# Top-32 attention and a cosine-gated feed-forward layer on one core: feed-forward blocks of 128 tokens, shared PSUM banks, mask and Exp first in ScalarE's slot

## The chip, the cores and the metric

The kernel runs on one NeuronCore of a Trainium2 chip. The core has five engines that run side by side, each through its own instructions in order: TensorE (PE: matmuls; its weight loads are listed as PEld), VectorE (DVE), ScalarE (ACT), GpSimd (POOL) and SyncE (SP, which here issues DMAs). They wait for each other through semaphores. The metric is the device time of one execution in microseconds, the median of several runs.

## What is computed

Eight batches of eight heads, 576 queries and keys of 64 dimensions. Of each row of scores the 32 largest go through a softmax, the others count as zero. The output of all heads, as 4608 tokens of 512 features, goes through a layer of 2048 hidden units that are gated by their own cosine. All data are float32.

```python
def _attn_ref(q, k, v):                      # (8, 8, 576, 64)
    scores = scale * np.matmul(q, k.transpose(0, 1, 3, 2))
    kth = np.partition(scores, -top_k, axis=-1)[..., -top_k:-top_k + 1]
    scores = np.where(scores >= kth, scores, -1000000000.0)
    scores = scores - np.max(scores, axis=-1, keepdims=True)
    attn = np.exp(scores)
    attn = attn / (np.sum(attn, axis=-1, keepdims=True) + 1e-09)
    return np.matmul(attn, v).astype(np.float32)

def _moe_ref(x, w_in, w_out):                # (4608, 512), (512, 2048), (2048, 512)
    h = x @ w_in
    g = h * np.cos(h)
    return (g @ w_out).astype(np.float32)
```

## The kernel before

**Units and slots.** The tokens of all batches stand in a row and are cut into 36 tiles of 128. A unit is one such tile for one pair of heads, so there are 4 x 36 = 144 units, four to a tile (`units`). A tile that crosses from one batch to the next has two `parts`. The main loop runs slot by slot: slot i does the top-k of unit i on VectorE, and other steps for its neighbours. Slots 0 to 8 are written in `early_slot`, the others in `slot`. The kernel is scheduled by hand: each engine runs its instructions in the order in which the code issues them.

**A unit's way.** `scores` (L206) makes 2 x 128 x 576 scores on TensorE in four PSUM banks (`sc`), one slot ahead; `take_scores` (L216) copies them to `s` on ScalarE. `topk_round` (L230, L233) finds eight maxima at a time on VectorE, four rounds for each head. One slot later `bounds`, `mask` and `exponentials` (L241, L244, L253, L261, L266) run on ScalarE: everything below the 32nd value is pushed far down, Exp is taken and its sum goes to `den`. In the slot after that `reciprocal` (L270) stands first on VectorE, and GpSimd normalises (L275) and splits the words into halves (L287), which SP writes to DRAM (L292). One slot later SP issues a DMA that reads them back transposed into `pT` (L298), and one slot later still `values` (L333) multiplies by V on TensorE into the bank `o`, and `take_values` (L340) copies the result to `xT` on ScalarE. The first eight units are transposed on TensorE instead (`transposes_now`, L310, with copies L314 and L317).

**Feed-forward.** `widths` cuts the tokens into blocks: four of 128, fifteen of 256, two of 128. When all units of a block are through, its products may start. A call of `ff1` (L381) makes 256 columns of the first product in a bank `mm`: for a block of 256 one group of hidden units, for one of 128 two groups. Each matmul of the program is two instructions in the trace. When a bank is full, `take_first` (L393) copies it to `g` on ScalarE. The cosine is taken as a sine: GpSimd reduces the argument (L419 to L428), ScalarE takes the sine (L438, with a table load when Exp was last), and GpSimd multiplies (`gate`, L445). A call of `ff2` (L457) adds two groups of hidden units to a bank `o` of its own (`o2`), which `take_second` (L466) copies to `ob` for the output's DMA. Which calls stand in a slot is decided when the program is built, by `feed`: four credits a slot, alternating between the two products, if their inputs were issued early enough.

**PSUM.** Eight banks: four for `sc`, two that take turns for `mm`, one for `o` and one for `o2`.

**Weights.** They come as chunks of 64-bit words that are decoded on ScalarE (L126 to L128), VectorE (L137, L138) and GpSimd (L147, L148) in the first slots.

**The end.** After the last unit four more slots let it pass through, and a last loop feeds what is left of the products; there VectorE takes over the reduction and the gate.

Of the kernel before, what the change touches and what calls it, by code (L numbers as in the profile page):

```python
# [17 lines left out]
P = 128  # L18
# [13 lines left out]
def kernel(  # L32
# [58 lines left out]
    for f in range(NF):  # L91
        w = consts.tile([P, DM], F32, tag=f"w_out{f}", name=f"w_out{f}")
        w_out.append(w)
        chunks.append((moe_w_out[f * P : (f + 1) * P, :], w))
    CHUNKS, XB = 8, 4
    ff = {"live": 0, "tick": 0, "now": 0, "credit": 0.0, "end": False, "kind": 0}
# [205 lines left out]
    def transposes_now(u):  # L302

        s = u.pop("s").rearrange("p j k -> p (j k)")
        tp = ps.tile([P, 2, 2, 512], F32, tag="sc", name="tp", bufs=1)
        tt = ps.tile([P, 512], F32, tag="ot", name="tt", bufs=1)
        for c in range(2 * NT + 1):
# [11 lines left out]
    def values(u):  # L319

        pT = u.pop("pT")
        o = u["o"] = ps.tile([P, 512], F32, tag="ot", name="o", bufs=1)
        for b, _, rows, r0 in u["parts"]:
            st = pairs[b, u["hp"]]
            r = slice(r0, r0 + rows)
            for c in range(NT + 1):
                for j in range(2):
                    d = slice(j * D, (j + 1) * D)
                    if c < NT:
                        lhsT, rhs = st["v"][:, c, d], pT[:, j * (NT + 1) + c, r]  # L330
                    else:
                        lhsT, rhs = st["v_tail"][:, d], pT[:, NT, r]
                    nc.tensor.matmul(o[d, r], lhsT, rhs, start=c == 0, stop=c == NT)  # L333

    def take_values(u):
        blk = block_of[u["tok"]]
        if "xT" not in blk:
            blk["xT"] = work.tile([P, NP, blk["w"]], F32, tag="xT", name="xT", bufs=4)
        at = u["tok"] - blk["t0"]
# [3 lines left out]

    widths = [P] * 4 + [2 * P] * (B * S // (2 * P) - 3) + [P] * 2
    assert sum(widths) == B * S
    blocks, block_of = [], {}
# [20 lines left out]
    def ff1(blk, i):  # L367
# [6 lines left out]
        if part % 2 == 0:  # L374
            blk["mm"] = ps.tile([P, 512], F32, tag="mm", name="mm")
        g, mm = blk["g"][-1], blk["mm"]
# [71 lines left out]
    def ff2(blk, i, f0):  # L448
        w = blk["w"]
        if f0 == 0:  # L450
            blk["o"] = ps.tile([P, 512], F32, tag="o2", name="o2", bufs=1)
        o = blk["o"]
# [71 lines left out]

    EARLY = 2 * NP

    def early_slot(i, u, w):
        n = 3 if i < 6 else 2
        decode_second()
        topk_round(u, 0)  # L530
# [9 lines left out]
        topk_round(u, 1)  # L540
        topk_round(u, 2)
        topk_round(u, 3)
        decode_third(1)
# [9 lines left out]
        if i != NP:  # L553
            decode_first(n - 1)
        feed(2)
        if w:
            transposes_now(w)
        decode_first(n - len(wq["second"]))
        if w:
            values(w)  # L560
            take_values(w)
        sines(2)

    def slot(i, u, w, x, y, z):
        decode_second()
        if x:
            reciprocal(x)
        if u:
            for rnd in range(TOPK // 8):
                topk_round(u, rnd)  # L570
        take_banks()
# [14 lines left out]
        if x:  # L586
            normalise(x)
            split(x)
            write_halves(x)
        if w:  # L590
            bounds(w)
            mask(w)
            exponentials(w)
        feed(2)
        take_banks()
        decode_third(2)
        decode_first(2)
        reduce_first()
        reduce_second()
        feed(4)  # L600
        sines(2)

    tt = ps.tile([P, 512], F32, tag="ot", name="warm", bufs=1)
    for _ in range(8):
# [7 lines left out]
    decode_first(3)  # L612
    for i in range(NU + 4):
        ff["end"] = i >= NU
        ff["credit"] = min(ff["credit"] + 4.0, 5.0)
        ff["now"] += 1
        wq["ready"] = wq["done"]
        u, w = (units[i - n] if 0 <= i - n < NU else None for n in range(2))
        x, y, z = (units[i - n] if EARLY <= i - n < NU else None for n in range(2, 5))
        if i <= EARLY:  # L620
# [50 lines left out]
```

## Time and profile before

| | us |
|---|---|
| runs before (3) | median 1688.67, 1683.35 to 1691.39 |
| the profiled execution | 1690.27 |
| its span, first to last instruction | 1688.4 |
| TensorE busy | 1483.0 (88%) |
| VectorE busy | 1457.4 (86%) |
| ScalarE busy | 1110.4 (66%) |
| GpSimd busy | 1100.0 (65%) |
| mean granted TensorE clock | 0.935 of 2.4 GHz |

The profile lists each instruction with its start and length, and for an idle stretch of an engine the instruction elsewhere that ended it. Two engines are busy for most of the span, so a share of busy time alone doesn't tell which of them sets the pace: that is read from who waits for whom in the stretch where the kernel spends most of its time. Matmuls are pipelined, and a busy TensorE is therefore not one at its peak; what a group of matmuls costs is read from the start of the group to the start of the next. TensorE's clock has two levels, 1.2 and 2.4 GHz, and the granted clock of a stretch is given as a share of the higher one.

### The profile page before, as it was taken

To read this page: it belongs to the slowest core of one execution; us is meant where nothing else is said; L and a number is where in the kernel's file an instruction comes from. 1 tells how busy PE (TensorE), PEld (TensorE's weight loads), DVE (VectorE), ACT (ScalarE), POOL (GpSimd) and SP (SyncE) were. 2 spreads that over 40 slices of the span, in tenths; PEclk is the share of its full clock that TensorE was granted. 3 is DMA by queue.
4 is the path that set the end of the run, shared out by engine and by line. 5 is a ranking of instruction groups with operands and counts; after the bars stand their busy time and mean duration, and the time that the engine had idled before them with its cause. 6 is when DMAs were issued, how large, how long until landed. Compare 5 with 4: busy or idle time off the path is not lost.

```text
span 1688.4 us, 24574 instructions
## 1 busy us (share of the span) xinstructions
PE 1483.0 (88%) x8400; PEld 967.1 (57%) x8400; DVE 1457.4 (86%) x3107; ACT 1110.4 (66%) x2200; POOL 1100.0 (65%) x835
## 2 busy tenths in 40 slices
PE   4658679797989999999999989999999999999998
PEld 2546356373646565656565646565656565656674
DVE  6999998899899898989898988989898989898620
ACT  7878657566667676767676766666676767676520
POOL 5787666476486767676767676767676767676600
PEclk9689789797999999999999999999999999999999
DMA  8422464435544465546454355544553454443500
GB/s 258 134 76 80 119 161 132 129 114 165 140 132 121 105 175 140 140 105 175 136 144 118 106 145 150 146 119 133 147 147 107 129 149 133 120 127 111 134 13 19
DMA packets 381502, 216.57 MB, mean 128 GB/s; under 512 B 330688, under 2 KB 347073, under 8 KB 381377
## 3 DMA queue, kind: packets, MB, share of 16 engines
q1 hardware_dynamic: 381216, 214.84, 46.3%
q8 instruction: 66, 1.08, 0.3%
q14 instruction: 60, 0.48, 0.1%
q10 hardware_dynamic: 160, 0.16, 0.0%
HBM read 45.09 MB, written 89.65 MB: 80 GB/s over the span
## 4 chain that ended last, share of the span: by engine, by line
PE 67%; ACT 14%; DVE 6%; DMA 4%; POOL 4%; issue 3%; SPq 2%; ACTq 0%; POOLq 0%; DVEq 0%
PE o L457 26%; PE mm L381 23%; PE o L333 10%; PE sc L206 8%; DMA pT<-rows 4%; ACT s L261 3%; ACT s L253 3%; DVE m L230 3%; ACT s L216 2%; DVE rest L233 2%; ACT ob L466 1%; ACT nd L244 1%; POOL g L445 1%; POOL halves L287 1%; POOL x L428 1%
## 5 line engine op out<-in xcount | busy, mean ns | idle before, releaser
L457 PE MATMUL o<-w_out,g 128*128 128x512 f32 x1152 | 592.3, 652 | 110.7 <-ACT ob L466 81.9
L230 DVE MAX8 m<-rest 128x8 f32<-128x576 f32 x864 | 609.4, 747 | 0.0
L381 PE MATMUL mm<-xT,w_in 128*128 128x256 f32 (+1 forms) x2688 | 544.7, 355 | 9.0 <-ACT xT L340 4.6
L381 PEld LDWEIGHTS mm<-xT,w_in 128*128 128x128 f32 x2688 | 458.8, 194 | 143.5 <-issue 86.8
L457 PEld LDWEIGHTS o<-w_out,g 128*128 128x128 f32 x1152 | 224.8, 206 | 374.1 <-issue 250.7
L233 DVE MATCH_REPLACE8 rest<-m,rest 128x576 f32<-128x576 f32 x576 | 423.4, 743 | 0.0
L275 POOL TENSOR_SCALAR s<-s,rden 128x576 f32<-128x576 f32 x288 | 212.1, 749 | 166.4 <-DVE rden L270 164.5
L287 POOL COPY halves<-s 128x2304 uint16<-128x2304 uint16 x136 | 285.9, 2102 | 30.9 <-DMA rows<-halves 23.6
L445 POOL TENSOR_TENSOR g<-g,x 128x1024 f32<-128x1024 f32 x65 | 153.7, 2365 | 219.3 <-ACT x L438 219.2
L216 ACT COPY s<-sc 128x1152 f32<-128x1152 f32 x144 | 161.1, 1119 | 125.5 <-PE sc L206 117.1
L261 ACT ACTIVATE s<-s,nd 128x576 f32<-128x576 f32 x288 | 219.3, 762 | 0.6
L233 DVE MATCH_REPLACE8 rest<-m,s 128x576 f32<-128x576 f32 x288 | 211.6, 743 | 0.0
L333 PE MATMUL o<-pT,v 128*64 128x128 f32 (+1 forms) x2560 | 170.0, 278 | 40.6 <-DMA pT<-rows 26.2
L253 ACT ACTIVATE s<-s,nb 128x576 f32<-128x576 f32 x288 | 205.3, 760 | 0.0
L230 DVE MAX8 m<-s 128x8 f32<-128x576 f32 x288 | 201.7, 742 | 0.0
L206 PE MATMUL sc<-k,q 64*128 64x288 f32 (+1 forms) x1280 | 192.1, 447 | 7.7 <-DMA k<-in_k_dram 7.6
L333 PEld LDWEIGHTS o<-pT,v 128*64 128x64 f32 x2560 | 135.3, 143 | 108.2 <-issue 64.2
L340 ACT COPY xT<-o 128x128 f32<-128x128 f32 x144 | 37.9, 263 | 240.6 <-PE o L333 240.6
L393 ACT ACTIVATE g<-mm 128x512 f32<-128x512 f32 x144 | 84.1, 586 | 128.9 <-PE mm L381 128.9
L428 POOL TENSOR_TENSOR x<-g,x 128x1024 f32<-128x1024 f32 x67 | 158.3, 2363 | 5.6
L270 DVE RECIPROCAL rden<-den 128x2 f32<-128x2 f32 x144 | 22.3, 155 | 131.8 <-ACT den L266 131.8
L206 PEld LDWEIGHTS sc<-k,q 64*128 64x128 f32 (+1 forms) x1280 | 104.3, 185 | 53.1 <-issue 18.6
(48 smaller groups left out, 1059.7 us busy)
## 6 DMA issues: line engine op xcount, KB each, us to landing
rows<-halves SPq DMA_DIRECT2D x136, 576.0 KB, 3.1
q<-in_q_dram SPq DMA_DIRECT2D x32, 288.0 KB, 3.1
out_dram<-ob SPq DMA_DIRECT2D x36, 256.0 KB, 2.7
st<-in_moe_w_in_dram SPq DMA_DIRECT2D x16, 512.0 KB, 6.2
v<-in_v_dram SPq DMA_DIRECT2D x32, 256.0 KB, 3.0
st<-in_moe_w_out_dram SPq DMA_DIRECT2D x16, 512.0 KB, 3.3
k<-in_k_dram SPq DMA_DIRECT2D x31, 144.0 KB, 3.3
k<-in_k_dram SPq DMA_DIRECT2D x32, 128.0 KB, 3.7
```

Of the source, the lines that this page charges most:

```text
L206: nc.tensor.matmul(sc[r0 : r0 + rows, j, h, 0:HS], st["q"][d, q0 : q0 + rows], st["k"][d, h * HS : (h + 1) * HS], start=True, stop=True,)
L216: nc.scalar.copy(out=s.rearrange("p j (h w) -> p (j h) w", h=2), in_=u.pop("sc").rearrange("p j h w -> p (j h) w")[:, :, 0:HS],)
L230: nc.vector.max(m8[:, j, at], src[:, j])
L233: nc.vector.match_replace(rest[:, j], m8[:, j, at], src[:, j], NEG)
L253: nc.scalar.activation(out=s[:, j], in_=s[:, j], func=AF.Prelu, bias=nb[:, j, 1:2], scale=SCALE, alpha=FAR)
L261: nc.scalar.activation(out=s[:, j], in_=s[:, j], func=AF.Exp, bias=nd[:, j : j + 1], scale=1.0, accum_out=den[:, j : j + 1],)
L275: nc.gpsimd.tensor_scalar(out=s[:, j], in0=s[:, j], scalar1=rden[:, j : j + 1], scalar2=1.0, op0=ALU.mult, op1=ALU.mult,)
L287: nc.gpsimd.tensor_copy(out=halves, in_=s.rearrange("p (k h) -> p h k", h=2))
L333: nc.tensor.matmul(o[d, r], lhsT, rhs, start=c == 0, stop=c == NT)
L381: nc.tensor.matmul(mm[:, at : at + w], w_in[f // FC][:, c, (f % FC) * P : (f % FC + 1) * P], blk["xT"][:, c], start=c == 0, stop=c == NC - 1,)
L428: nc.gpsimd.tensor_tensor(out=x, in0=g, in1=x, op=ALU.subtract)
L457: nc.tensor.matmul(o, g[:, at : at + P], w_out[f], start=f == 0, stop=f == NF - 1)
```

## The change

All feed-forward blocks are 128 tokens wide. The PSUM banks of `mm`, `o`, `o2` and of the ninth transpose (`tt`) come from one group of four. In `slot`, mask and Exp of the last unit stand after the first round of the top-k, so first on ScalarE. The last four units (from `LAST`) are masked, normalised, transposed on TensorE and multiplied with V in one slot, and the main loop ends three slots earlier. A slot's credits are 4.1, and its last call of `feed` is for one call. There are nine buffers for `g` and staged weights, and five for `xT`. In `early_slot` the decoding on VectorE in slot 0 comes after the third round, and `feed` stands after the transposes.

```diff
@@ -92,7 +92,7 @@
         w = consts.tile([P, DM], F32, tag=f"w_out{f}", name=f"w_out{f}")
         w_out.append(w)
         chunks.append((moe_w_out[f * P : (f + 1) * P, :], w))
-    CHUNKS, XB = 8, 4
+    CHUNKS, XB = 9, 4
     ff = {"live": 0, "tick": 0, "now": 0, "credit": 0.0, "end": False, "kind": 0}
 
     wq = {"next": 0, "loaded": deque(), "second": deque(), "third": deque(), "done": 0, "ready": 0}
@@ -303,7 +303,7 @@
 
         s = u.pop("s").rearrange("p j k -> p (j k)")
         tp = ps.tile([P, 2, 2, 512], F32, tag="sc", name="tp", bufs=1)
-        tt = ps.tile([P, 512], F32, tag="ot", name="tt", bufs=1)
+        tt = ps.tile([P, 512], F32, tag="mm", name="tt", bufs=4)
         for c in range(2 * NT + 1):
             j, k = divmod(c, NT + 1)
             to = tt[:, 0:P] if c == NT else tp[:, 0, j, k * P : (k + 1) * P]
@@ -319,7 +319,7 @@
     def values(u):
 
         pT = u.pop("pT")
-        o = u["o"] = ps.tile([P, 512], F32, tag="ot", name="o", bufs=1)
+        o = u["o"] = ps.tile([P, 512], F32, tag="mm", name="o", bufs=4)
         for b, _, rows, r0 in u["parts"]:
             st = pairs[b, u["hp"]]
             r = slice(r0, r0 + rows)
@@ -335,14 +335,13 @@
     def take_values(u):
         blk = block_of[u["tok"]]
         if "xT" not in blk:
-            blk["xT"] = work.tile([P, NP, blk["w"]], F32, tag="xT", name="xT", bufs=4)
+            blk["xT"] = work.tile([P, NP, blk["w"]], F32, tag="xT", name="xT", bufs=5)
         at = u["tok"] - blk["t0"]
         nc.scalar.copy(out=blk["xT"][:, u["hp"], at : at + P], in_=u.pop("o")[:, 0:P])
         blk["left"] -= 1
 
 
-    widths = [P] * 4 + [2 * P] * (B * S // (2 * P) - 3) + [P] * 2
-    assert sum(widths) == B * S
+    widths = [P] * (B * S // P)
     blocks, block_of = [], {}
     t0 = 0
     for w in widths:
@@ -372,7 +371,7 @@
             blk["g"].append(ffw.tile([P, 1024], F32, tag="g", name="g", bufs=CHUNKS))
             ff["live"] += 1
         if part % 2 == 0:
-            blk["mm"] = ps.tile([P, 512], F32, tag="mm", name="mm")
+            blk["mm"] = ps.tile([P, 512], F32, tag="mm", name="mm", bufs=4)
         g, mm = blk["g"][-1], blk["mm"]
         for a in range(nf):
             f = i * nf + a
@@ -448,7 +447,7 @@
     def ff2(blk, i, f0):
         w = blk["w"]
         if f0 == 0:
-            blk["o"] = ps.tile([P, 512], F32, tag="o2", name="o2", bufs=1)
+            blk["o"] = ps.tile([P, 512], F32, tag="mm", name="o2", bufs=4)
         o = blk["o"]
         per = 1024 // w
         for f in range(f0, f0 + 2):
@@ -522,11 +521,12 @@
 
 
 
-    EARLY = 2 * NP
+    EARLY, LAST = 2 * NP, NU - NP
 
     def early_slot(i, u, w):
         n = 3 if i < 6 else 2
-        decode_second()
+        if i > 0:
+            decode_second()
         topk_round(u, 0)
         scores(units[i + 1])
         for load, b, hp in at_slot.get(i, []):
@@ -539,6 +539,8 @@
             reciprocal(w)
         topk_round(u, 1)
         topk_round(u, 2)
+        if i == 0:
+            decode_second()
         topk_round(u, 3)
         decode_third(1)
         if w:
@@ -552,22 +554,34 @@
         reduce_second()
         if i != NP:
             decode_first(n - 1)
-        feed(2)
         if w:
             transposes_now(w)
+        feed(1)
         decode_first(n - len(wq["second"]))
         if w:
             values(w)
             take_values(w)
+        feed(2)
         sines(2)
 
     def slot(i, u, w, x, y, z):
+        now = w and i - 1 >= LAST
         decode_second()
         if x:
             reciprocal(x)
         if u:
-            for rnd in range(TOPK // 8):
-                topk_round(u, rnd)
+            topk_round(u, 0)
+        if w:
+            bounds(w)
+            mask(w)
+            exponentials(w)
+        if u:
+            topk_round(u, 1)
+            topk_round(u, 2)
+        if now:
+            reciprocal(w)
+        if u:
+            topk_round(u, 3)
         take_banks()
         if z:
             values(z)
@@ -587,20 +601,23 @@
             normalise(x)
             split(x)
             write_halves(x)
-        if w:
-            bounds(w)
-            mask(w)
-            exponentials(w)
         feed(2)
         take_banks()
         decode_third(2)
         decode_first(2)
+        if now:
+            normalise(w)
         reduce_first()
         reduce_second()
-        feed(4)
+        feed(2)
+        if now:
+            transposes_now(w)
+            values(w)
+            take_values(w)
+        feed(1)
         sines(2)
 
-    tt = ps.tile([P, 512], F32, tag="ot", name="warm", bufs=1)
+    tt = ps.tile([P, 512], F32, tag="mm", name="warm", bufs=4)
     for _ in range(8):
         nc.tensor.transpose(tt[:, 0:P], ident, ident)
     load_qk(0, 0)
@@ -610,13 +627,13 @@
     scores(units[0])
     take_scores(units[0])
     decode_first(3)
-    for i in range(NU + 4):
+    for i in range(NU + 1):
         ff["end"] = i >= NU
-        ff["credit"] = min(ff["credit"] + 4.0, 5.0)
+        ff["credit"] = min(ff["credit"] + 4.1, 5.0)
         ff["now"] += 1
         wq["ready"] = wq["done"]
         u, w = (units[i - n] if 0 <= i - n < NU else None for n in range(2))
-        x, y, z = (units[i - n] if EARLY <= i - n < NU else None for n in range(2, 5))
+        x, y, z = (units[i - n] if EARLY <= i - n < LAST else None for n in range(2, 5))
         if i <= EARLY:
             early_slot(i, u, w)
         else:
```

On TensorE in the steady part, the slot in which a second product ends or starts. `sc` are the scores, `mm` the first product, `o_8085<-w_out` a second product (`o` with a number), `o<-pT,v` P@V. Before:

```order
L333 MATMUL o<-pT,v 64x128 x8
L333 MATMUL o<-pT,v_tail_116 64x128 x2
L206 MATMUL sc<-k,q 128x288 x4
L457 MATMUL o_7771<-w_out_104,g 128x512
L457 MATMUL o_7771<-w_out_105,g 128x512
L457 MATMUL o_8085<-w_out_90,g 128x512
L457 MATMUL o_8085<-w_out_91,g 128x512
L457 MATMUL o_8085<-w_out_92,g 128x512
L457 MATMUL o_8085<-w_out_93,g 128x512
```

After the change:

```order
L333 MATMUL o<-pT,v 64x128 x8
L333 MATMUL o<-pT,v_tail_112 64x128 x2
L206 MATMUL sc<-k,q 128x288 x4
L380 MATMUL mm<-xT,w_in_86 128x128 x16
L456 MATMUL o_8218<-w_out_90,g 128x512
L456 MATMUL o_8218<-w_out_91,g 128x512
L380 MATMUL mm<-xT,w_in_87 128x128 x8
L456 MATMUL o_8218<-w_out_92,g 128x512
L456 MATMUL o_8218<-w_out_93,g 128x512
```

Where one second product followed directly on another, two calls of the first product of a new block now stand between the scores and the start of the next second product.

On ScalarE in the steady part, around the copy of a finished second product to `ob`. Before:

```order
L340 COPY xT<-o 128x128
L216 COPY s<-sc 128x1152
L241 ACTIVATE nb<-m_5715 128x4
L244 ACTIVATE nd<-m_5715,nb 128x1 x2
L253 ACTIVATE s<-s,nb 128x576 x2
L261 ACTIVATE s,den<-s,nd 128x576 x2
L266 ACTIVATE den<-den,eps 128x2
L466 ACTIVATE ob<-o_5545 128x512
L393 ACTIVATE g<-mm 128x512
```

After the change:

```order
L216 COPY s<-sc 128x1152
L437 ACT_TABLE_LOAD
L437 ACTIVATE x<-x,halfpi 128x1024
L241 ACTIVATE nb<-m_6345 128x4
L244 ACTIVATE nd<-m_6345,nb 128x1 x2
L253 ACTIVATE s<-s,nb 128x576 x2
L261 ACT_TABLE_LOAD
L261 ACTIVATE s,den<-s,nd 128x576 x2
L266 ACTIVATE den<-den,eps 128x2
L465 ACTIVATE ob<-o_6146 128x512
L340 COPY xT<-o 128x128
L216 COPY s<-sc 128x1152
```

The group from `nb` to `den` stood behind `xT` and `s` of its slot and now stands ahead of them; `ob` and `xT` follow on it.

On VectorE, the start of the program. Before:

```order
L69 MEMSET eps 128x1
L137 TENSOR_SCALAR w_in_86<-w_in_86 128x512
L138 TENSOR_SCALAR w_in_86<-w_in_86 128x512
...
L230 MAX m_171<-s 128x8 x2
L233 MATCH_REPLACE rest<-m_171,s 128x576 x2
```

After the change:

```order
L69 MEMSET eps 128x1
L230 MAX m_165<-s 128x8 x2
L233 MATCH_REPLACE rest<-m_165,s 128x576 x2
L230 MAX m_165<-rest 128x8 x2
L233 MATCH_REPLACE rest<-m_165,rest 128x576 x2
...
L137 TENSOR_SCALAR w_in_86<-w_in_86 128x512
```

The decoding of the first weights (three pairs of L137 and L138) moved behind the third round of unit 0.

## Rows read from the trace of the kernel before

**Rows 1.** Stretch, length, busy PE PEld DVE ACT POOL, granted clock, DMA share, GB/s.

```profile
236.00:1583.00 1347.00, 1226.36 (x6922) 790.50 (x6923) 1226.83 (x2645) 913.61 (x1817) 925.67 (x685) 0.95 0.49 134
```

**Rows 2.** Timeline of VectorE: start, duration, instruction, [idle before <-what ended it].

```profile
760.03 0.17 DVE L270 RECIPROCAL rden<-den 128x2 f32<-128x2 f32 x1 [6.04 <-ACT den L266]
...
1554.08 1.40 DVE L230 MAX8 m<-s 128x8 f32<-128x576 f32 x2
...
1563.78 1.40 DVE L230 MAX8 m<-s 128x8 f32<-128x576 f32 x2
```

**Rows 3.** Waits, 236 to 1583 us: total, times, longest; VectorE's, then TensorE's.

```profile
DVE rden L270 <- ACT den L266: 120.1, 49, 6.9
...
PE o L457 <- ACT ob L466: 71.7, 26, 3.8
PE o L333 <- DMA pT<-rows: 26.0, 14, 7.2
```

**Rows 4.** Timeline around 750 us, ScalarE's rows and then TensorE's.

```profile
742.16 0.58 ACT L466 ACTIVATE ob<-o 128x512 f32<-128x512 f32 x1
742.76 1.28 ACT L438 ACT_TABLE_LOAD   x1
744.05 1.15 ACT L438 ACTIVATE x<-x,halfpi 128x1024 f32<-128x1024 f32 x1
752.36 0.27 ACT L340 COPY xT<-o 128x128 f32<-128x128 f32 x1 [7.16 <-PE o L333]
753.59 1.12 ACT L216 COPY s<-sc 128x1152 f32<-128x1152 f32 x1 [0.96 <-PE sc L206]
754.60 0.21 ACT L241 ACTIVATE nb<-m 128x4 f32<-128x4 f32 x1
...
759.63 0.30 ACT L266 ACTIVATE den<-den,eps 128x2 f32<-128x2 f32 x1
...
742.88 8.19 PE L457 MATMUL o<-w_out,g 128*128 128x512 f32 x12 [3.73 <-ACT ob L466]
751.00 1.09 PE L333 MATMUL o<-pT,v 128*64 128x128 f32 x16
...
753.41 1.13 PE L457 MATMUL o<-w_out,g 128*128 128x512 f32 x2
```

**Rows 5.** Same view as rows 1, stretches after idles of TensorE.

```profile
417.00:427.00 10.00, 9.98 (x45) 5.60 (x46) 9.42 (x20) 2.30 (x6) 3.44 (x3) 0.83 0.75 232
...
1562.10:1572.10 10.00, 9.98 (x53) 6.53 (x54) 10.00 (x23) 4.59 (x11) 6.28 (x5) 1.00 0.67 146
742.90:749.70 6.80, 6.80 (x10) 2.94 (x11) 6.80 (x16) 2.29 (x2) 6.16 (x5) 0.59 0.76 128
```

**Rows 6.** First and second product in TensorE's timeline, and weight loads by form.

```profile
761.18 8.90 PE L381 MATMUL mm<-xT,w_in 128*128 128x256 f32 x40
...
1618.10 3.73 PE L381 MATMUL mm<-xT,w_in 128*128 128x128 f32 x32
1621.67 1.88 PE L457 MATMUL o<-w_out,g 128*128 128x512 f32 x4
1623.39 1.95 PE L381 MATMUL mm<-xT,w_in 128*128 128x128 f32 x16
...
L381 PEld LDWEIGHTS mm<-xT,w_in 128*128 128x128 f32 x2688 | 458.8, 194 | 143.5 <-issue 86.8 <-ACT g L393 6.1 <-ACT xT L340 4.9
```

**Rows 7.** The last of 16 gaps of TensorE of 1.86 to 2.05 us.

```profile
1562.12 1.98 PE L457 MATMUL o<-w_out,g 128*128 128x512 f32 x4 [1.91 <-ACT ob L466]
```

**Rows 8.** Start of the timeline: first copy to s, first MAX8.

```profile
8.76 1.12 ACT L216 COPY s<-sc 128x1152 f32<-128x1152 f32 x1 [5.53 <-PE sc L206]
...
15.31 1.42 DVE L230 MAX8 m<-s 128x8 f32<-128x576 f32 x2
```

**Rows 9.** Unit 0 on its way over TensorE: normalising, copy to xT.

```profile
30.37 1.47 POOL L275 TENSOR_SCALAR s<-s,rden 128x576 f32<-128x576 f32 x2 [0.15 <-DVE rden L270]
...
37.33 0.27 ACT L340 COPY xT<-o 128x128 f32<-128x128 f32 x1 [0.60 <-PE o L333]
```

## Prediction

> **What bounds the kernel now.** I read the windows first, then the waits, then one stretch of the timeline. Between 236 and 1583 us, 80% of the span, two engines are near full: TensorE is busy 1226.4 and VectorE 1226.8 of 1347 us; ScalarE and GpSimd, at 913.6 and 925.7, are not [rows 1]. A slot is the work between the top-k of one unit and that of the next; VectorE needs 9.70 us for it when it waits for nothing (first MAX8 at 1554.08 and 1563.78) [rows 2]. Its idle time in that stretch has one cause: 120.1 us in 49 waits of the reciprocal for ScalarE's `den` [rows 3]; the large ones are like that of 6.04 us at 760.03 [rows 2]. Spread over the 124 slots of the stretch that is 7.7 us for a block of eight. So VectorE sets the pace, and something behind `den` takes a tenth from it.
>
> What that is stands in the timeline. TensorE stops 3.73 us ahead of L457 (row at 742.88), because the bank of the second product is single and its copy to `ob` stands on ScalarE behind the exponentials (742.16). The next 12 matmuls take 8.19 us [rows 4], and the granted clock in that stretch is 0.59 of 2.4 GHz, so mostly at the lower level [rows 5]. P@V, queued behind them, comes at 751.00; ScalarE, in order, has waited 7.16 us for it ahead of `xT`, and starts the exponentials only then: `den` ends at 759.93, where VectorE has waited 6.04 us [rows 2, 4].
>
> **The change: the end of that wait.** With mask and Exp first in ScalarE's slot, `den` of a unit is ready most of a slot before its reciprocal, so the 120.1 us go. With four banks in common the second product no longer waits for `ob` (71.7 us of TensorE's waits in the same stretch [rows 3]). What is late next decides the time, so I work out the new loop of four slots (a block is now 128 tokens, four units).
>
> TensorE's terms, from rows at the full clock: a call of the first product on 128 tokens is 16 matmuls, 1.79 us (32 of them from 1618.10 to 1621.67: 3.57); a call of the second is 1.72 (1621.67 to 1623.39) [rows 6]; P@V and scores together take 2.41 (751.00 to 753.41) [rows 4]; I count 0.1 for each change over to P@V. The narrow products cost nothing to speak of: two matmuls of 128 columns take 223 ns, one of 256 takes 222 (40 in 8.90 us) [rows 6]. A block is 8 x 1.79 + 8 x 1.72 + 4 x 2.41 + 0.4 = 38.1 us; VectorE needs 4 x 9.70 = 38.8. Neither exceeds the other by much, so the order on ScalarE decides.
>
> By that order the first call of a block's first product waits for `xT` of its last unit, copied on ScalarE behind Exp and `ob`. Call the start of that call 0. TensorE then runs without a stop: the rest of this slot 3.57 + 1.72 + 1.79 + 1.82 = 8.9; the second slot 2.41 + 1.79 + 1.72 + 1.79 + 1.82 = 9.5; the third 2.41 + 3.57 + 1.72 + 1.89 = 9.6; P@V and scores of the fourth 2.4. That is 30.4. From there ScalarE has a chain: 0.18 to see the scores and 1.12 for `s` (753.41, 753.59), 2.44 for table load and sine (742.76 to 745.20), 5.33 from `nb` to `den` with Exp's own table load (754.60 to 759.93), 0.58 for `ob`, 0.27 for `xT` [rows 4]: 9.9, and with two hand-overs of some 0.05 the next block begins at **40.4 us**. VectorE waits 40.4 - 38.8 = 1.6 us a block, now for `s`. TensorE meanwhile does three calls (5.26) and the next P@V and scores (2.41): done at 38.1, it idles some 2.2 us a block. From slot 20 to 139 there are 30 blocks: 30 x 1.6 = 48 us in place of 120, **-72 us**.
>
> **The clock on those idles.** TensorE's clock fell after some idles of this size. There are 16 gaps of 1.86 to 2.05 us between 417 and 1562 us (the last is shown) [rows 7]; after 5 of them, the first among these, the granted clock over the next 10 us was 0.83, after the other 11, the last among these, 1.00 [rows 5]. 0.83 over 10 us is 1.7 us of work lost, and here all of it lies in the loop. An idle of 2.2 us is a little longer, and shorter than the one of 3.73 that cost more (0.59 over 6.8 us: 2.8). I take half of the 30 followed by such a stretch: 15 x 1.7 = **+26 us**; the ends are 0 and 30 x 2.8 = 84.
>
> **Smaller terms.** *Start:* VectorE's first MAX8 is at 15.31 because three weight decodings stand ahead of it, though the copy to `s` began at 8.76 and takes 1.12 [rows 4, 8]. They now come behind the third round, when their inputs are long there: **-5 us** (0 to -5.4). *Transposes on the DMA queue:* SP issues them behind loads of q, k and v that wait for scores or P@V of the same slot. TensorE waited 26.0 us for `pT` in 14 places [rows 3], and the loop gives it less slack than before: **+5 us** (0 to +26). *End:* units 140 to 143 are now transposed on TensorE. From normalising to `xT` this way took 7.2 us for unit 0 (30.37 to 37.60) [rows 9], and Exp takes 5.3, or 4.0 without the table load [rows 4]; since ScalarE is in order, the Exp of the next unit stands behind the last copy of this one, so the chains follow on each other instead of overlapping. From the start of the last top-k but one (1563.78) I get about +23 us to the end of the second chain, +31 to the first product of the block before the last (TensorE has idled near 8 us by then, so a slow stretch of 3 to 5 us is counted), +61 to the end of the last chain, then by the order 11 calls of the first product and 20 of the second, 54 us, and 4 for the last `ob` and its DMA: 119. Before it was 1688.4 - 1563.8 = 124.6 [rows 2]. Behind the last scores stand 12 calls of the second product and 6 of the first less, but most of that comes back as waits in those chains: **-5 us** (-15 to +10). More buffers for `g` and `xT` cost nothing, and in the new order a bank's last reader stands at least a slot ahead of its next writer.
>
> Sum against the profiled execution's own 1690.3 (span 1688.4; the median shown is 1688.7): 1690.3 - 72 + 26 - 5 + 5 - 5 = **1639**.
>
> **A rule that speaks against narrow blocks.** The rows have 128-column matmuls at 112 ns each, with a new weight load for each [rows 6]. The Trainium skill, TensorE: Matmul & The Clock Gate, section Back-to-back issue gap, has it that in a stream of load and matmul pairs both set the pace, 81 ns for 128 columns where the matmul alone would take 56; by that rule narrow blocks cost more than in proportion, and rival (e) is what it would make here. The trace so far disagrees: its narrow calls run in proportion, loads included.
>
> **Rivals.** *(a) No idle brings the clock down, and the loop holds:* 1639 - 26 = 1613. *(b) The loop closes better than I have it and VectorE alone sets the pace, 9.70 a slot:* 1690 - 120 - 10 = 1560; against it, sine, Exp and `ob` all lie in ScalarE's queue between the scores and `xT`. *(c) The wait moves to `pT`:* 56 slots of the stretch carry loads ahead of the transpose on SP; at the 1.9 us of a wait for `pT` before (26.0 in 14) [rows 3], 24 of them make 45 us in place of my 5: 1679, at the edge of what a measurement can tell from no change. *(d) Slower, by the clock:* every block's idle is followed by a half-clock stretch that costs the loop 3.4 us (one of 6.8 us in full): 30 x 3.4 = 102 in place of 26, 1715. It decides from 2.6 us a block: there 30 x 2.6 = 78 eats the 72 and the small terms. For it speaks that the idle comes back at the same place in every block; against it, 11 of 16. *(e) Weight loads set the pace:* 458.8 us busy for 2688 loads is 171 ns each [rows 6]; at 171 in place of 112 the 128 matmuls of a block have 7.6 us more, 30 x 7.6 = 228: some 1865. The paired narrow calls near the end of the trace speak against it.
>
> **Chances.** The forecast 0.46, (a) 0.17, (b) 0.05, (c) 0.15, (d) 0.13, (e) 0.02, other 0.02. A measurement here tells about 0.5%, 8.4 us, from no change. Faster takes nearly all of the forecast, (a), (b) and a part of (c): 0.74; within 0.5%: 0.11; slower, (d) with (e): 0.15. The likeliest case alone spans 1613 to 1670. The range goes from 1595, past (a) toward (b), to 1700, short of (d)'s centre: some 2 in 10 are left out.
>
> **What would show it.** VectorE's waits for `den` gone, and waits for `s` in their place, 1 to 3 us a block; slots of 9.7 to 10.5 us; TensorE idle about 2 us once a block, ahead of the first product, for `xT`, and the granted clock after it at 1.00 in about half of the cases; first MAX8 near 10 us; 32 matmuls of 128 columns still in 3.6 us. If `pT` leads TensorE's waits, (c) is right; if the mean granted clock between 236 us and the last top-k falls below 0.93, (d). I am wrong altogether if slots stay near 10.7 us, or if the last top-k ends early and what follows takes far more than 124 us.

## The result and the profile after

The changed kernel takes 1586.95 us (median of four runs, 1585.37 to 1588.86), the kernel before on the same chip 1688.97. The ratio is 0.940, with an interval of 0.9375 to 0.9427: 102 us faster, where the prediction said 50. The direction was right, the size was not, and 1587 lies below the stated range.

The profiled execution of after took 1585.37 us with a span of 1583.5. Its windows over the steady part; columns as in [rows 1]:

```profile
253.00:1452.00 1199.00, 1163.57 (x8589) 821.25 (x8588) 1170.57 (x2519) 912.66 (x1767) 892.52 (x660) 1.00 0.53 143
```

Its waits over the same stretch (total, times, longest), GpSimd's, VectorE's and TensorE's, which answer to [rows 3]:

```profile
POOL halves L287 <- DMA rows<-halves: 165.6, 59, 6.0
...
DVE m L230 <- ACT s L216: 29.7, 62, 1.7
...
PE mm L380 <- ACT xT L340: 23.7, 25, 2.1
...
PE o L333 <- DMA pT<-rows: 10.9, 10, 2.0
```

VectorE is now busy 98% of the stretch (1170.57 of 1199) in place of 91%. Its waits for `den` (120.1 us) are gone, and so is TensorE's wait for `ob` (71.7). In their place stand 29.7 us of short waits for `s`. The granted clock is 1.00; in before, the clock records from 253 to 1452 us hold 23 pieces at the lower level. GpSimd's long wait for its write to DRAM stands in neither list of the two full engines: what of it reaches TensorE can only lie in the 10.9 us of waits for `pT`.

One block in the timeline of after. First ScalarE, then TensorE (start, duration, instruction, [idle before <- what ended it]), and VectorE's first instruction of four slots in a row; it answers to [rows 4] and [rows 2]:

```profile
690.02 1.28 ACT L261 ACT_TABLE_LOAD   x1
...
692.98 0.29 ACT L266 ACTIVATE den<-den,eps 128x2 f32<-128x2 f32 x1
693.18 0.58 ACT L465 ACTIVATE ob<-o 128x512 f32<-128x512 f32 x1
693.66 0.25 ACT L340 COPY xT<-o 128x128 f32<-128x128 f32 x1
693.80 1.13 ACT L216 COPY s<-sc 128x1152 f32<-128x1152 f32 x1
...
690.90 1.24 PE L206 MATMUL sc<-k,q 64*128 64x288 f32 x8
692.07 0.94 PE L380 MATMUL mm<-xT,w_in 128*128 128x128 f32 x6
693.97 3.17 PE L380 MATMUL mm<-xT,w_in 128*128 128x128 f32 x26 [0.96 <-ACT xT L340]
696.97 1.88 PE L456 MATMUL o<-w_out,g 128*128 128x512 f32 x4
...
733.66 3.17 PE L380 MATMUL mm<-xT,w_in 128*128 128x128 f32 x26 [0.96 <-ACT xT L340]
...
706.02 1.42 DVE L230 MAX8 m<-s 128x8 f32<-128x576 f32 x2 [0.25 <-ACT s L216]
716.26 1.42 DVE L230 MAX8 m<-s 128x8 f32<-128x576 f32 x2 [0.44 <-ACT s L216]
725.99 1.40 DVE L230 MAX8 m<-s 128x8 f32<-128x576 f32 x2
735.68 1.41 DVE L230 MAX8 m<-s 128x8 f32<-128x576 f32 x2
```

The loop is the one that the prediction drew: once a block TensorE waits for `xT`, which stands on ScalarE behind Exp and `ob`. But its period is 733.66 - 693.97 = 39.7 us, not 40.4, and the idle 0.96, not 2.2. The reason for the shorter period stands in the row at 692.07. Each sum of the first product runs over four head pairs, and `xT` of three of them is old. Six of the first call's 16 matmuls are therefore done before the last copy comes, and only 10 are left to do at what the prediction called 0. Six matmuls at 112 ns are 0.67 us, which is the whole difference between 40.4 and 39.7. It is half of the difference between the idles; the rest is TensorE's own work, 39.7 - 0.96 = 38.7 us a block where the prediction's sum had 38.1.

Where the 104.9 us between the two spans come from, by the start of slots (first MAX8 of a unit) in the two traces:

| stretch | before | after | difference | predicted |
|---|---|---|---|---|
| start to unit 12 | 171.7 | 174.0 | +2.2 | -5 (start) |
| unit 12 to 20 | 87.5 | 79.0 | -8.5 | not counted |
| unit 20 to 140 | 1285.1 | 1199.2 | -85.9 | -41 (-72 +26 +5) |
| unit 140 to the end | 144.0 | 131.3 | -12.7 | -5 |

### The profile page after: what moved, and what is told of

Same layout as the page of the kernel before. It is cut to its first block, busy times and chain, and to the rows that moved or that the text cites. A ratio compares the mean times of both kernels' runs of the same rounds, so it can differ in the third digit from the quotient of the medians.

```text
span 1583.5 us, 28533 instructions
## 1 busy us (share of the span) xinstructions
PE 1448.9 (92%) x10356; PEld 1024.1 (65%) x10356; DVE 1461.5 (92%) x3103; ACT 1155.6 (73%) x2244; POOL 1101.0 (70%) x837
## 4 chain that ended last, share of the span: by engine, by line
PE 66%; ACT 18%; DVE 9%; DMA 3%; SPq 1%; issue 1%; POOL 0%; ACTq 0%; POOLq 0%; DVEq 0%
PE mm L380 29%; PE o L456 19%; PE o L333 9%; PE sc L206 8%; DVE m L230 4%; DVE rest L233 3%; ACT s L261 3%; DMA pT<-rows 3%; ACT s L253 3%; ACT L437 2%; ACT L261 2%; ACT x L437 2%; ACT s L216 2%; ACT ob L465 1%; ACT nd L244 1%
## 5 line engine op out<-in xcount | busy, mean ns | idle before, releaser
L380 PEld LDWEIGHTS mm<-xT,w_in 128*128 128x128 f32 x4608 | 546.2, 193 | 130.7 <-issue 91.8
L380 PE MATMUL mm<-xT,w_in 128*128 128x128 f32 x4608 | 572.3, 279 | 33.1 <-ACT xT L340 33.1
L456 PE MATMUL o<-w_out,g 128*128 128x512 f32 x1152 | 535.9, 598 | 7.3 <-POOL w_out L148 7.0
L287 POOL COPY halves<-s 128x2304 uint16<-128x2304 uint16 x132 | 277.5, 2102 | 176.7 <-DMA rows<-halves 172.3
L456 PEld LDWEIGHTS o<-w_out,g 128*128 128x128 f32 x1152 | 203.3, 191 | 198.5 <-issue 187.9
L230 DVE MAX8 m<-s 128x8 f32<-128x576 f32 x288 | 203.2, 747 | 39.7 <-ACT s L216 39.6
L333 PE MATMUL o<-pT,v 128*64 128x128 f32 (+1 forms) x2560 | 173.3, 276 | 37.4 <-DMA pT<-rows 27.2
L206 PE MATMUL sc<-k,q 64*128 64x288 f32 (+1 forms) x1280 | 188.9, 443 | 10.1 <-ACT s L216 6.1
L444 POOL TENSOR_TENSOR g<-g,x 128x1024 f32<-128x1024 f32 x67 | 158.9, 2372 | 14.8 <-ACT x L437 14.8
L418 POOL TENSOR_SCALAR x<-g 128x1024 f32<-128x1024 f32 x68 | 71.3, 1049 | 128.5 <-ACT g L392 119.5
## 6 DMA issues: line engine op xcount, KB each, us to landing
k<-in_k_dram SPq DMA_DIRECT2D x31, 144.0 KB, 3.4
```

The costliest lines, as they stand in the source:

```text
L206: nc.tensor.matmul(sc[r0 : r0 + rows, j, h, 0:HS], st["q"][d, q0 : q0 + rows], st["k"][d, h * HS : (h + 1) * HS], start=True, stop=True,)
L230: nc.vector.max(m8[:, j, at], src[:, j])
L287: nc.gpsimd.tensor_copy(out=halves, in_=s.rearrange("p (k h) -> p h k", h=2))
L380: nc.tensor.matmul(mm[:, at : at + w], w_in[f // FC][:, c, (f % FC) * P : (f % FC + 1) * P], blk["xT"][:, c], start=c == 0, stop=c == NC - 1,)
L456: nc.tensor.matmul(o, g[:, at : at + P], w_out[f], start=f == 0, stop=f == NF - 1)
```

## The experiments

The theory to be tested: the prediction's loop is right, and what it missed is that the block's first product starts ahead of its last input; the short idle that this leaves is also why the clock holds. The rival: the loop is set by something else, and the clock held by chance. A second pair concerns what ended the waits for `den` at all: the prediction named mask and Exp first and the shared banks; the rival is that narrow blocks alone would do.

**late_first.** The changed kernel, with each sum of the first product started on the head pair that is finished last:

```diff
-            for c in range(NC):
+            for n, c in enumerate((3, 0, 1, 2)):
...
-                    start=c == 0,
-                    stop=c == NC - 1,
+                    start=n == 0,
+                    stop=n == NC - 1,
```

> The changed kernel, but each sum of the first product takes the last head pair first, so the first matmul of a block needs the copy to xT that comes last. Theory (three of the four head pairs run before that copy): 6 matmuls, 0.67 us, no longer fill the gap; TensorE's idle ahead of a block grows from 0.96 to about 1.6 us, a block from 39.7 to 40.3 us, VectorE's waits for s between 253 and 1452 us from 29.7 to about 50, time about 1607; up to 1625 if some of the longer idles are followed by a lower clock. Rival (the loop was only shorter because ScalarE's instructions overlap, the order of the sums doesn't matter): 1587, idle 0.96 as before.

**late_first_ob2.** The same, and `ob` is copied twice, which puts one more copy into the chain:

```diff
         nc.scalar.mul(out=ob, in_=o, mul=2.0 * math.pi)
+        nc.scalar.mul(out=ob, in_=o, mul=2.0 * math.pi)
```

> As late_first, and the copy to ob made twice, 0.58 us more on ScalarE ahead of xT once a block. Theory: TensorE idles 2.2 us once a block, the size that the prediction took; a block 40.9 us; without a lower clock 1587 + 34 x 1.25 = 1630, with a lower clock of 1.7 us lost after half of the idles, as the prediction had it, about 1655. If idles of 2.2 us always bring the clock down: 1690 and more. Rival (order of the sums irrelevant): idle 1.5, 1607, no lower clock.

Measured: 1625.22 us, ratio 0.9635 (0.9612 to 0.9657), for the first, and 1639.66, 0.9713 (0.9671 to 0.9754), for the second. Waits of late_first, 253 to 1452 us, then two of its block starts and the windows just behind each:

```profile
DVE m L230 <- ACT s L216: 59.1, 61, 3.4
PE mm L380 <- ACT xT L340: 44.0, 24, 3.1
```

```profile
663.59 3.84 PE L380 MATMUL mm<-xT,w_in 128*128 128x128 f32 x32 [1.71 <-ACT xT L340]
...
703.96 5.46 PE L380 MATMUL mm<-xT,w_in 128*128 128x128 f32 x32 [1.82 <-ACT xT L340]
```

```profile
705.00:713.00 8.00, 8.00 (x47) 7.00 (x46) 8.00 (x19) 3.51 (x9) 2.99 (x4) 0.79 0.75 165
664.00:672.00 8.00, 8.00 (x54) 6.39 (x54) 8.00 (x18) 4.87 (x12) 3.57 (x4) 1.00 0.75 219
```

All 32 matmuls now stand behind the wait, and the period is 703.96 - 663.59 = 40.4 us, that of the prediction. Most blocks of this run have it; those behind a drop of the clock, as at 703.96 (5.46 us in place of 3.84, granted 0.79 from 705 to 713), have 42.0, so a drop costs 1.6 us where the prediction had 1.7. Of the 37 us between the profiled executions of this run and of after, 30 lie between unit 20 and 140, where the loop gives 20 (30 x 0.67) and eight drops at 1.6 us some 13; the time lies at the upper end of what was expected. Two block starts of late_first_ob2:

```profile
881.12 3.84 PE L380 MATMUL mm<-xT,w_in 128*128 128x128 f32 x32 [2.45 <-ACT xT L340]
...
922.11 3.84 PE L380 MATMUL mm<-xT,w_in 128*128 128x128 f32 x32 [2.45 <-ACT xT L340]
```

With the second copy the undisturbed block takes 41.0 us and the idle is 2.45; the time lies between the 1630 and the 1655 expected without drops and with a drop after every second idle. That it equals the prediction's 1639 is chance: the loop is longer than the predicted one and the drops are fewer. The loop theory stands, and the order of four terms in a sum is worth 38 us here.

**exp_last.** The changed kernel with mask and Exp back behind the copies, but for the last four units:

```diff
-        if w:
+        if now:
             bounds(w)
             mask(w)
             exponentials(w)
...
+        if w and not now:
+            bounds(w)
+            mask(w)
+            exponentials(w)
```

> The changed kernel with mask and Exp back behind the copies of their slot, for all units but the last four. Theory (Exp first is what took the waits for den away): the reciprocal waits again for den, 2 to 4 us a block of four; 1630 to 1690. Rival (the narrow blocks and the shared banks did it, since they took away TensorE's stop for ob): waits for den stay under 30 us in all, 1585 to 1605.

**own_banks.** The changed kernel with the banks of before: two for `mm`, one for `o`, one for `o2` (five `ps.tile` lines, of which two stand here).

```diff
-        o = u["o"] = ps.tile([P, 512], F32, tag="mm", name="o", bufs=4)
+        o = u["o"] = ps.tile([P, 512], F32, tag="ot", name="o", bufs=1)
...
-            blk["o"] = ps.tile([P, 512], F32, tag="mm", name="o2", bufs=4)
+            blk["o"] = ps.tile([P, 512], F32, tag="o2", name="o2", bufs=1)
```

> The changed kernel with the PSUM banks as in the kernel before: two for the first product, one for P@V and the ninth transpose, one for the second product. Theory of the prediction (the shared banks took 71.7 us of TensorE's waits for ob away): these come back in part, 1610 to 1650. Rival (in the new order ob is copied ahead of xT and the first product's first two calls stand ahead of the next second product, so the single bank is free in time): no wait for ob over 5 us in all, 1583 to 1593.

Measured: 1586.52 (0.9377 to 0.9415) and 1592.71 (0.9413 to 0.9456), both within 0.5% of after. VectorE's waits over 253 to 1452 us, of exp_last and then of own_banks, here with the first of TensorE's:

```profile
DVE rden L270 <- ACT den L266: 31.2, 38, 3.7
```

```profile
DVE m L230 <- ACT s L216: 31.2, 63, 1.7
...
PE mm L380 <- ACT xT L340: 22.7, 24, 2.2
```

With Exp last the waits are for `den` again, but only 31.2 us of them, as much as after has for `s`. The loop is then another one: TensorE has no wait for `xT` left, half of the blocks take 39.1 us and the others up to 43. With the single bank no wait for `ob` came back. So with narrow blocks in place neither part is what ended the 120 us of the steady part. Ahead of it Exp first does count: from unit 12 to 20 VectorE waits 6.2 us for `den` in exp_last, which takes 84.1 us there, and not at all in after, which takes 79.0; by the end of the run that lead is gone.

**b_narrow.** The kernel before with one line changed:

```diff
-    widths = [P] * 4 + [2 * P] * (B * S // (2 * P) - 3) + [P] * 2
+    widths = [P] * (B * S // P)
```

> The kernel before with blocks of 128 tokens throughout and nothing else. Theory R (the stop for ob and the slow clock behind it are the loss, and either narrow blocks or shared banks alone take them away): waits for den in the steady part fall from 120 to about 30 us, 1600 (the end stays as before, some 10 us behind the changed kernel). Rival N (narrow blocks need the other edits too, since Exp still stands behind the copies): 1640 to 1690.

**b_banks.** The kernel before with the four shared banks alone (the five `ps.tile` lines of the change, of which two stand here):

```diff
-        o = u["o"] = ps.tile([P, 512], F32, tag="ot", name="o", bufs=1)
+        o = u["o"] = ps.tile([P, 512], F32, tag="mm", name="o", bufs=4)
...
-            blk["o"] = ps.tile([P, 512], F32, tag="o2", name="o2", bufs=1)
+            blk["o"] = ps.tile([P, 512], F32, tag="mm", name="o2", bufs=4)
```

> The kernel before with the four PSUM banks in common and nothing else; blocks of 256 stay. Theory R: no wait for ob, waits for den from 120 to 20 to 50 us, 1595 to 1625. Rival (only narrow blocks help, because in a wide block eight slots bring calls of one product in a row and the copies to g or xT then hold TensorE): 1650 to 1690, TensorE's waits move from ob to another copy.

**wide.** The changed kernel with the widths and the numbers of buffers of before:

```diff
-    widths = [P] * (B * S // P)
+    widths = [P] * 4 + [2 * P] * (B * S // (2 * P) - 3) + [P] * 2
...
-    CHUNKS, XB = 9, 4
+    CHUNKS, XB = 8, 4
...
-            blk["xT"] = work.tile([P, NP, blk["w"]], F32, tag="xT", name="xT", bufs=5)
+            blk["xT"] = work.tile([P, NP, blk["w"]], F32, tag="xT", name="xT", bufs=4)
```

> The changed kernel with the widths of before (four blocks of 128, fifteen of 256, two of 128), with eight buffers for g and four for xT so that it fits. Theory R: 1590 to 1615, as the shared banks alone suffice. Rival (only narrow blocks help): 1650 to 1690.

Measured: b_narrow 1563.62 (0.9235 to 0.9294), b_banks 1571.82 (0.9283 to 0.9327), wide 1579.10 (0.932 to 0.937). All three beat the changed kernel, by 23, 15 and 8 us (the last just outside the intervals), and all three came out below the least that even the theory expected (1600, 1595 and 1590). Waits over 253 to 1452 us, of b_narrow, of b_banks and (one line) of wide:

```profile
DVE rden L270 <- ACT den L266: 24.3, 40, 2.6
...
PE o L333 <- DMA pT<-rows: 13.6, 12, 2.0
PE o L457 <- POOL g L445: 9.2, 29, 0.3
```

```profile
DVE rden L270 <- ACT den L266: 15.9, 11, 3.3
...
PE o L457 <- POOL g L445: 31.9, 17, 7.5
PE o L333 <- DMA pT<-rows: 10.7, 8, 4.0
```

```profile
DVE m L230 <- ACT s L216: 7.6, 7, 1.7
```

Either narrow blocks alone or shared banks alone removes the wait for `ob`, the slow stretch behind it and most of the waits for `den` (b_banks keeps slow stretches behind waits for `g` and `pT` before 490 us, as before has them). b_narrow shows how, in TensorE's and ScalarE's timeline:

```profile
683.69 3.60 PE L457 MATMUL o<-w_out,g 128*128 128x512 f32 x8
...
689.63 3.94 PE L381 MATMUL mm<-xT,w_in 128*128 128x128 f32 x32
693.40 1.88 PE L457 MATMUL o<-w_out,g 128*128 128x512 f32 x4
...
689.62 0.58 ACT L466 ACTIVATE ob<-o 128x512 f32<-128x512 f32 x1
```

In before, a block of 256 has two second products, the second behind the first on the same bank [rows 4]. Narrow blocks always have the new block's first product between them: here 3.94 us of it, and `ob`, copied at 689.62, is long done when the bank is wanted at 693.40. That is the pair of order pieces shown ahead of the prediction for TensorE; it was read there as a fact of the order, not as the cure. Narrow blocks bring a second gain at the end: of before's work, 155 matmuls of the second product and 304 of the first stand behind the last scores in the trace, of b_narrow's 107 and 256. That is 12 and 6 calls, 31 us at 1.72 and 1.79, and from unit 140 to the end b_narrow takes 111.7 us in place of 144.0.

The steady part says the opposite. From unit 20 to 140 wide takes 1172.4 us and b_banks 1177.8, close to the 1164 that VectorE needs; after takes 1199.2 and b_narrow 1191.2. So narrow blocks cost 27 us there in the changed kernel (after against wide, which also has one buffer less of `g` and of `xT`) and win 22 at the end (131.3 against 153.7). With Exp last, b_narrow_banks_start against b_banks (their starts differ too), it is 13 lost and 25 won. In the changed kernel most of the loss is the wait that the loop brings once in four slots: VectorE's waits for `s` are 29.7 us, in wide 7.6. Wide blocks in the steady part and narrow ones only at the end, with shared banks, were not run.

**end_dma.** The changed kernel with the last four units on the way of all others:

```diff
-    EARLY, LAST = 2 * NP, NU - NP
+    EARLY, LAST = 2 * NP, NU
...
-    for i in range(NU + 1):
+    for i in range(NU + 4):
```

> The changed kernel with its last four units transposed by DMA and three more slots, as before. From the start of unit 140's top-k to the end took 144.0 us before and 131.3 in the changed kernel. Theory (the transposes on TensorE are worth these 12.7 us): 1600. Rival (the gain at the end comes from less work left over): 1587, or less, since the three chains in a row with an idle of 6.69 us on TensorE go.

Measured: 1573.86 (0.9293 to 0.934), 13 us better than after; from unit 140 to the end 118.3 us in place of 131.3, though the same 107 and 256 matmuls are left. So the transposes on TensorE are not worth the 12.7 us of the end, as the theory of 1600 had it; they cost 13. The end of after, VectorE, then TensorE, and the windows over the gap:

```profile
1485.55 0.17 DVE L270 RECIPROCAL rden<-den 128x2 f32<-128x2 f32 x1 [4.36 <-ACT den L266]
```

```profile
1493.43 0.94 PE L380 MATMUL mm<-xT,w_in 128*128 128x128 f32 x6
1501.06 4.50 PE L380 MATMUL mm<-xT,w_in 128*128 128x128 f32 x26 [6.69 <-ACT xT L340]
...
1524.82 3.84 PE L380 MATMUL mm<-xT,w_in 128*128 128x128 f32 x32
```

```profile
1495.00:1505.00 10.00, 3.94 (x23) 3.94 (x24) 2.04 (x4) 5.92 (x14) 3.82 (x3) 0.66 0.08 28
```

The chains follow on each other on ScalarE, as forecast: TensorE idles 6.69 us for one of them, with the clock down behind it (0.66 from 1495 to 1505), and by 1524.82 all four have passed. On the way over the queue the same place shows one idle of 2.13 us:

```profile
1493.45 4.64 PE L380 MATMUL mm<-xT,w_in 128*128 128x128 f32 x26 [2.13 <-ACT xT L340]
```

**ob_after_xt.** The changed kernel with `take_banks`, and so `ob`, behind `take_values`: the chain ahead of `xT` loses 0.5 us.

```diff
-        take_banks()
         if z:
             values(z)
...
             take_values(z)
+        take_banks()
```

> The changed kernel with the copies out of full banks of a slot (ob, g) behind those to xT and s, so that 0.58 us go from ScalarE's chain ahead of a block's first product. Theory (in the steady part a loop of TensorE and ScalarE of 39.7 us a block sets the pace, VectorE needs 38.8): a block 39.1, TensorE's idle for xT under 0.5 us, waits for s between 253 and 1452 us from 29.7 to about 13, time 1570. Rival (TensorE alone is full and sets the pace): no gain, 1582 to 1592.

Measured: 1579.99 (0.9334 to 0.9384), 7 us better, with intervals that still overlap; 1570 was expected, and the loop alone (30 x 0.5 us) would give twice as much. Its block start and waits:

```profile
691.78 3.17 PE L380 MATMUL mm<-xT,w_in 128*128 128x128 f32 x26 [0.47 <-ACT xT L340]
```

```profile
DVE m L230 <- ACT s L216: 28.4, 44, 2.4
...
PE o L333 <- DMA pT<-rows: 15.1, 14, 2.3
PE mm L380 <- ACT xT L340: 12.1, 23, 1.7
```

The plain block went to 39.2 us and the idle to 0.47, as the loop has it. But the waits for `pT` rose from 10.9 to 15.1 us, and a third of the blocks, those in which TensorE waits for `pT` or that follow one, take 40.2 to 42.3. So part of what one chain gave went to the next late one; the steady part as a whole is 3 us shorter.

**start_r1.** The changed kernel with the decoding of slot 0 one round earlier; **b_narrow_start**, the same start in b_narrow; **b_narrow_banks_start**, with the shared banks as well.

```diff
         topk_round(u, 1)
-        topk_round(u, 2)
         if i == 0:
             decode_second()
+        topk_round(u, 2)
         topk_round(u, 3)
```

> The changed kernel with the decoding of the first weights on VectorE behind the second round of unit 0 in place of the third. Theory (behind the third round it lets GpSimd's part of the decoding run beside VectorE's decoding of slot 1, whose instructions then take 1.4 to 1.5 us in place of 0.42): slot 1 starts at 23 to 25 us in place of 30.1, time 1580 to 1582. Rival (slot 1 is late because its copy to s is): 30, 1587.

> The kernel before with blocks of 128 tokens, and the decoding of slot 0 behind the second round of unit 0. Theory: slot 1 starts at 23 to 25 us in place of 27.4, all later work moves with it, 1559 to 1561. Rival (the early slots wait for weights or loads anyway): 1563.

> As b_narrow_start, and the four banks in common. Theory R (narrow blocks alone already took the wait for ob away): same time as b_narrow_start within 5 us. Rival (the banks add to it): 1545 to 1555.

Measured: 1586.21, 1565.38 and 1561.57 us (0.9249, 0.9223 to 0.9275, for the last); none is told apart from the kernel that it starts from. The theory had 1580 to 1582 and 1559 to 1561 for the first two, a gain hardly larger than what these intervals can tell. In the trace of start_r1 unit 1 begins 4.2 us earlier than in after, and unit 20 still does. By unit 140 1.2 us are left, and at the end 0.1. What took them is not shown: the steady part is the same code in end_dma, which took 1201.9 us there, start_r1 1202.3, after 1199.2, so 3 us may be no more than what executions differ by. In b_narrow_start unit 0 begins at 10.62 in place of 15.33 and unit 1 at 28.08 in place of 27.36, so there the gain is lost on the spot. Why stands in the start of after, VectorE with GpSimd beside it:

```profile
10.48 1.42 DVE L230 MAX8 m<-s 128x8 f32<-128x576 f32 x2 [9.59 <-ACT s L216]
...
18.81 0.42 DVE L137 TENSOR_SCALAR w_in<-w_in 128x512 f32<-128x512 f32 x1
...
23.04 1.39 DVE L138 TENSOR_SCALAR w_in<-w_in 128x512 int32<-128x512 int32 x1
24.12 1.46 POOL L147 TENSOR_TENSOR w_in<-w_in,st 128x512 int32<-128x512 int32 x1
24.36 1.51 DVE L137 TENSOR_SCALAR w_in<-w_in 128x512 f32<-128x512 f32 x1
25.66 1.35 POOL L148 TENSOR_TENSOR w_in<-w_in,st 128x512 f32<-128x512 f32 x1
...
30.06 1.41 DVE L230 MAX8 m<-s 128x8 f32<-128x576 f32 x2
```

The first MAX8 came 4.83 us earlier, as predicted. But the decoding, done in a wait for its weights before, now takes VectorE's time, and GpSimd's part of it now falls beside the next decoding on VectorE. One decoding instruction takes 0.42 us at 18.81 and 1.4 to 1.5 beside GpSimd and ends some 0.3 us after GpSimd's that it began beside (24.43 after 24.15, 25.87 after 25.58). Unit 1 starts at 30.06 in place of 27.34. In before GpSimd's L147 and L148 ran beside MAX8, which kept its 1.41 us. The Trainium skill, SBUF — State Buffer, section Who interferes with whom, says that VectorE and GpSimd share one pair of ports under an exclusive lock, which VectorE's `tensor_scalar` may take and an instruction with one input outside the two-port modes does not. The trace agrees: the decoding's `tensor_scalar` went from 0.42 to 1.4 us and more, and MAX8, with one input, stayed at 1.41.

The best of all, b_narrow_banks_start at 1561.57, beats before by 7.5% and the changed kernel by 25 us, but can't be told from b_narrow, which is one line of the change.

## Why the prediction came out half as large as the gain

- **The end of the wait for `den` (-72): right in kind, too small, and credited to the wrong parts.** That the 120 us would go and short waits for `s` would come was right. The step that failed is the start of the loop: that the first call of a block's first product waits for `xT` of the last unit holds only from that call's seventh matmul on, the first that reads the last head pair. Over 30 blocks of 38.8 us VectorE's excess was 121 us before; 79 were forecast for after (48 by the loop, 26 by the clock, 5 for `pT`), and 35 remain: 26 by the loop (0.87 a block) and 9 for the rest, mostly `pT`. late_first puts the missing 0.67 us back and finds the predicted 40.4. TensorE's own work was also summed too low, 38.1 us a block for 38.7; that doesn't lengthen the loop, but it shortens the idle (1.8 us in late_first, where the prediction had 2.2).
- **The clock (+26): the largest single miss, and it follows from the same step in part.** The half-and-half guess was made for idles of 2.2 us; in after most are 0.96, and the term is 0. With the loop as predicted, in late_first, it is 13 (eight drops at 1.6), so the share of one half was itself too high there. The last section gives the share by length of idle. The prediction's 16 gaps are 17 in the trace: one of 1.89 us, at 490.49, was left out, and an idle of 3.56 follows close on it.
- **The parts of the change.** The prediction gave the end of the `den` waits to mask and Exp first, and that of the `ob` waits to the shared banks. exp_last and own_banks show that in the steady part neither is needed beside narrow blocks; b_narrow and b_banks show that narrow blocks or shared banks, each alone, do it. The wait for `den` was the shadow of the stop for `ob`. The prediction had read that chain correctly in its first part and then didn't ask which edits cut it.
- **Narrow products (0): right for the products.** In after 26 matmuls of 128 columns take 3.00 us to the next row (693.97 to 696.97), 115 ns each with a load for each. What narrow blocks do cost, the loop once in four slots, is most of 27 us of the steady part (wide), and the prediction didn't set it against the end.
- **The start (-5): wrong in sign.** Unit 12 is 2.2 us late. The first MAX8 was right; that GpSimd's decoding would meet VectorE's was not seen. What that costs at the end of the run is too small to be told: start_r1, 4 us earlier at unit 1, is not told apart from after.
- **Units 12 to 20 (-8.5): not counted.** The sum began at unit 20, though the waits for `den` begin earlier: before has 9.4 us of them from unit 12 to 20. Here it is Exp first that ends them: every run with Exp last keeps 6.2 us or more, and no run with Exp first has any.
- **The end (-5): -12.7.** The gap ahead of the first product of the block before the last came at +28.3 us from unit 142 (1501.06; forecast 31), the last chain was through at +52.0 (1524.82; forecast 61), and what follows took 58.7 (forecast 58). The chains were costed too long. The mechanism was right, and end_dma shows that it loses 13 us: the gain at the end is that of narrow blocks, which have less work left.
- **Rivals.** (a) named the clock rightly, (b) the loop in part: the truth lies between their 1613 and 1560. (c) to (e) didn't come. The four parts of the miss, +7 at the start, -8.5, -45 in the steady part (about -22 the loop, -26 the clock and +4 the rest) and -8 at the end, make the 54 us between 1639 and the profiled 1585.4.

Left open: why unit 140 to the end still takes 118.3 us in end_dma and 111.7 in b_narrow, with the same matmuls left; it wasn't followed further.

## What to carry to other kernels

Where a matmul sums over inputs that become ready one after another, put the last one last in the sum, and work a loop out from the first instruction that really waits: 0.67 us a block, and the drops of the clock that came with it, were worth 38 us here. When several edits aim at one stall, follow the stall back to the first engine that stops and ask of each edit alone whether it cuts that; here one line did more than all of the change. Read the steady part and the end apart: narrow blocks lost 27 us in the one and won 22 in the other.

## What the runs showed of the hardware that was not expected

Of TensorE's idles between 253 and 1452 us, those of 0.7 to 1.2 us were never followed by a stretch at 1.2 GHz in the rows close behind them (0 of 22 in after); of those of 1.7 to 2.1 us 7 of 24 were in late_first, 5 of 15 in before, 1 of 7 in late_first_ob2 and none of 4 in after; of 2.1 to 2.6 us 8 of 20 in late_first_ob2; of 2.6 us or more all 18 in before, but not the one of 2.92 us in wide (at 292.74). So the share is nought at 1 us and nearly all at 3, and between these the counts are too few for more than a third or so; one guess for "idles of this size" was a weak point of the sum.

One drop costs the loop 1.6 us: the block of 42.0 against 40.4 in late_first.

A decoding instruction of VectorE of 0.42 us takes 1.4 to 1.5 beside GpSimd's of 1.3, while GpSimd's own go to 1.35 to 1.47.
